# Attention followed by a feed-forward layer on one core: the attention output computed as token rows and transposed by TensorE, with a written-out program order

## The chip, the cores and the metric

The kernel runs on one core of one Trainium2 chip. The metric is device time in microseconds (us) of one execution. The kernel before takes 209.25 us, the median of three runs (209.20, 209.25 and 210.02 us).

## What is computed

The reference is a gated linear attention whose output goes through a feed-forward layer with a cosine gate. All arrays are float32: q, k, v and alpha have the shape (4, 8, 768, 48), that is 4 batches, 8 heads, 768 steps and 48 channels; w_in is 384 x 2048, w_out is 2048 x 384, and the result is 3072 x 384.

```python
for t in range(S):                                  # S = 768
    state = alpha[:, :, t, :, None] * state + einsum('bhd,bhe->bhde', k[:, :, t], v[:, :, t])
    y[:, :, t] = einsum('bhd,bhde->bhe', q[:, :, t], state)
x = y.transpose(0, 2, 1, 3).reshape(3072, 384)
h = x @ w_in
out = (h * cos(h)) @ w_out
```

## The kernel before

The 3072 tokens are cut into 24 chunks of 128; six chunks make one batch, and the attention state starts from nothing at chunks 0, 6, 12 and 18. Each chunk goes through the same small steps. The program has a one- or two-letter name for each step, and a string of such names with chunk numbers is the order in which the instructions of every engine are written. Each engine takes its own instructions strictly in that order, and waits where an operand or a buffer is not ready.

The steps of a chunk j are these. The names are used below.

- Loads on the SP queue: `a` (alpha), `k`, `q` and `v`, 192 KB each, in pieces of 192 bytes. Before, one step loads k and q together. `z` loads a part of w_in and `Z` a part of w_out.
- Decay: `l` (logarithm of alpha for two chunks, ACT), `C` (TensorE sums it along the chunk, L161 and L165), `E` (two exponentials, ACT, L179 and L181). `i`, `c` and `d` are the same for one chunk.
- Operands (GpSimd, shown as POOL): k times the inverse decay (L191, `khb`), q times the decay (L193, `qhb`), v cast to bfloat16 (L195, `vpb`), and a small decay mask (L197, `Em`). Before, one step `o` writes all four in this order.
- `T`: eight transposes of k and q on TensorE (L210); `t` copies them out of PSUM (DVE, L216).
- `A`: eight score matmuls, each on 48 rows of the array, alternately at row 0 and row 64 (L227); `m` masks them (DVE, L236).
- `S`: four matmuls for the chunk's contribution to the state (L249, 96 columns each); `u` adds the state before (DVE, L261) and multiplies by the decay (POOL, L263).
- `Y`: the attention output (L304). Before, the result is built transposed: v and the state are the weights, 64 columns of the array at a time, alternately in the left and the right half, and the scores or the transposed q stream through with 128 columns. That is 12 matmuls for the first chunk of a batch and 20 for the others. `y` copies the result out (DVE, L309) as `xT`, which the feed-forward layer reads.
- `F` and `G`: the two halves of x @ w_in, 24 matmuls each (L323); `f` and `g` the cosine on ACT (Sin of h + pi/2, L331); `p` and the gate of the second half multiply (DVE, L338).
- `V` and `W`: the two halves of the second matmul, 8 matmuls of 384 columns each (L347); `e` copies the result out (ACT, L363) and stores it.

PSUM has three pools. "big" has three buffers, of two banks each, for the sums of `C`, the scores and the halves `F` and `G`. "o" has one bank for the output of `V` and `W`. "g" has one single bank, which `T`, `S` and `Y` of every chunk use in turn, so that each of them waits until DVE has emptied the one before it:

```python
    def outputs(j):
        t = ps.tile([C, 512], FP, tag="g")
```

ACT holds either the table for logarithm and exponential or the one for Sin, and loads the other one when the order changes between them (L141 and L331).

The program has a written start (`START`, chunks 0 to 4) and then a loop with one fixed order per chunk. In the start, 63 matmuls on zeros (`warmup`, L370) fill waits of TensorE. w_in is loaded in two halves and w_out in two halves, and they are cast to bfloat16 by DVE (L121) and ACT (L119).

Of the kernel before, what the change touches and what calls it, by code (L numbers as in the profile page):

```python
# [9 lines left out]
FP = mybir.dt.float32  # L10
# [6 lines left out]
def kernel(  # L17
# [23 lines left out]
    VS = 112  # L41
# [4 lines left out]
    cpool = ctx.enter_context(tc.tile_pool(name="cpool", bufs=3))  # L46
# [55 lines left out]
    def load_qk(j):  # L102
        for nm, src, d in (("k_sb", k, k_t), ("q_sb", q, q_t)):
            t = inpool.tile([C, H, D], FP, tag=nm)
            nc.sync.dma_start(out=t, in_=rows(src, j))
            d[j] = t

    def load_v(j):
        t = inpool.tile([C, H, D], FP, tag="v_sb")
        nc.sync.dma_start(out=t, in_=rows(v, j))  # L110
        v_t[j] = t

    def load_w1(f0, f1):
        nc.sync.dma_start(out=w1f[:, :, f0:f1],
                          in_=moe_w_in[:, f0:f1].rearrange("(k p) f -> p k f", p=C))
# [7 lines left out]
    def cast_w1(half, eng, k0, k1):  # L123
        f = slice(half * (DF // 2), (half + 1) * (DF // 2))
        cast(eng, w1[:, k0:k1, f], w1f[:, k0:k1, f])

    def load_w2(f):
        nc.sync.dma_start(
            out=w2f[:, f : f + 8],
            in_=moe_w_out[f * C : (f + 8) * C, :].rearrange("(f p) n -> p f n", p=C),  # L130
        )

    def cast_w2(eng, f0, f1):
        cast(eng, w2[:, f0:f1], w2f[:, f0:f1])
# [52 lines left out]
    def operands(j, qeng):  # L187
        cp = cp_t[j // 2][:, j % 2]
        icp = icp_t[j // 2][:, j % 2]
        k_sb, q_sb, v_sb = k_t.pop(j), q_t.pop(j), v_t.pop(j)  # L190
        nc.gpsimd.tensor_tensor(out=khb[:, j % 3, :, 0:D], in0=k_sb,  # L191
                                in1=icp.rearrange("s (h d) -> s h d", h=H), op=ALU.mult)
        qeng.tensor_tensor(out=qhb[:, j % 3, :, 0:D], in0=q_sb,  # L193
                           in1=cp[:, 0:HD].rearrange("s (h d) -> s h d", h=H), op=ALU.mult)
        nc.gpsimd.tensor_copy(out=vpb[:, j % 3, :, 0:D], in_=v_sb)  # L195
# [75 lines left out]
    def outputs(j):  # L271
        t = ps.tile([C, 512], FP, tag="g")
        y_ps[j] = t
        first = j % NC == 0
        vs = vpb[:, j % 3].rearrange("s h e -> s (h e)")
        qT = qkT_t[j]

        U = ub[:, (j - 1) % 3].rearrange("r p e -> r (p e)")
        mms = []
        for T in range(2 * 3):  # L280
            g, tt = T // 3, T % 3
            a = []
            if not first:


                for p, c0 in (((0, 0),), ((0, 64), (1, 96)), ((1, 160),))[tt]:
                    c0 += 2 * C * g
                    a.append((U[:, c0 : c0 + 64],
                              qT[:, (NP + 2 * g + p) * C : (NP + 2 * g + p + 1) * C]))
            for r in range(2):  # L290
                h = 4 * g + (2 * tt + r + 1) // 2
                c0 = 4 * VS * g + 64 * (2 * tt + r)
                a.append((vs[:, c0 : c0 + 64], A_t[j][:, ACOL[h] * C : (ACOL[h] + 1) * C]))
            mms.append(a)
        for half in range(2):
            mms[half] = [
                (T // 2, i == 0, i == len(mms[T]) - 1) + m
                for T in range(half, 6, 2) for i, m in enumerate(mms[T])
            ]
        for i in range(max(len(mms[0]), len(mms[1]))):  # L300
            for half in range(2):
                if i < len(mms[half]):
                    kt, start, stop, lhsT, rhs = mms[half][i]
                    nc.tensor.matmul(t[64 * half : 64 * half + 64, kt * C : (kt + 1) * C],  # L304
                                     lhsT, rhs, start=start, stop=stop, skip_group_check=True)

    def ev_outputs(j):
        t = work.tile([C, 3, C], BF, tag="xT")
        nc.vector.tensor_copy(out=t.rearrange("r k t -> r (k t)"), in_=y_ps.pop(j)[:, 0 : 3 * C])  # L309
        x_t[j] = t  # L310
        qkT_t.pop(j)
        A_t.pop(j)

# [20 lines left out]
    def gate(j, half):  # L334
        if j not in g_t:
            g_new = moe.tile([C, NF, C], BF, tag="g_sb", bufs=4)
            g_t[j] = g_new
        nc.vector.tensor_tensor(out=g_t[j][:, half * HF : (half + 1) * HF],  # L338
                                in0=h_ps.pop((j, half)), in1=c_t.pop((j, half)), op=ALU.mult)

    def ff2(j, half, whole=True):
        if half == 0 or not whole:
            o_new = ps.tile([C, 512], FP, tag="g" if j == NCH - 1 else "o")
            o_ps[j] = o_new
        for f in range(HF):
            ft = half * HF + f
            nc.tensor.matmul(o_ps[j][:, 0:DM], g_t[j][:, ft], w2[:, ft],  # L347
                             start=(f == 0 and (half == 0 or not whole)),
                             stop=(f == HF - 1 and (half == 1 or not whole)))

    oh_t = {}

    def ev_first(j):
        oh = moe.tile([C, DM], FP, tag="oh", bufs=3)
        nc.scalar.activation(out=oh, in_=o_ps.pop(j)[:, 0:DM], func=AF.Copy)
        oh_t[j] = oh

    def ev_ff2(j):
        o_sb = moe.tile([C, DM], FP, tag="o_sb", bufs=3)
        if j in oh_t:  # L360
            nc.vector.tensor_tensor(out=o_sb, in0=o_ps.pop(j)[:, 0:DM], in1=oh_t.pop(j), op=ALU.add)
        else:
            nc.scalar.activation(out=o_sb, in_=o_ps.pop(j)[:, 0:DM], func=AF.Copy)  # L363
        g_t.pop(j)
        nc.sync.dma_start(out=out[j * C : (j + 1) * C, :], in_=o_sb)

    def warmup(n):
        w_ps = ps.tile([C, 512], FP, tag="o")
# [4 lines left out]
    dve, act_e, pool = nc.vector, nc.scalar, nc.gpsimd  # L373
    units = {

        "o": lambda j: operands(j, pool), "O": lambda j: operands(j, dve),
        "T": transposes, "t": ev_transposes, "S": state, "u": ev_state,
        "A": scores, "m": mask_scores, "Y": outputs, "y": ev_outputs,

        "F": lambda j: ff1(j, 0), "f": lambda j: act(j, 0), "p": lambda j: gate(j, 0),  # L380
        "G": lambda j: ff1(j, 1), "g": lambda j: act(j, 1), "q": lambda j: gate(j, 1),

        "V": lambda j: ff2(j, 0), "W": lambda j: ff2(j, 1, j not in oh_t), "e": ev_ff2,
        "X": lambda j: ff2(j, 0, False), "x": ev_first,

        "N": lambda g: lnset(), "l": lambda g: ln(2 * g, 2), "C": lambda g: cums(2 * g, 2),
        "E": lambda g: exps(2 * g, 2),
# [65 lines left out]
```

## Time and profile before

| | |
|---|---|
| median of three runs | 209.25 us |
| span of the profiled execution, first to last instruction | 208.2 us |
| time from the median that lies around the span | 1.05 us |
| instructions | 6187 |
| HBM read and written | 25.17 MB and 4.72 MB |
| TensorE matmuls at L323, L347, L304, L210, L227, L249 | 1152, 384, 448, 192, 192, 96 |

The profiled execution's own time is not listed beside its span, so the median of the runs stands for it. PE is TensorE's matmul side and PEld its weight loads, which overlap with matmuls. A busy time of PE counts matmuls that are in flight, so the distance between the starts of two neighbouring matmuls tells what one costs. In the profile most PSUM tiles are called "t".

### The profile page before, as it was taken

The numbers are of one execution on the slowest core, as the hardware profiler recorded it, in microseconds if no ns is written. First come the engines' busy times: TensorE is split into PE (matmuls) and PEld (weight loads), VectorE is DVE, ScalarE is ACT, GpSimd is POOL, SyncE is SP. The second block draws the span as 40 slices with busy tenths as digits, with TensorE's granted clock in tenths as the row PEclk, the third lists the DMA queues.
The fourth block names the chain that finished last, engine by engine and source line by source line (L and its number), as shares of the span: only waits on it lengthen the run. The fifth ranks groups of instructions, "written<-read, shape, count | busy, mean of one in ns | idle before, by whom it ended". The sixth has DMA issues, their size and how long they took to land.

```text
span 208.2 us, 6187 instructions
## 1 busy us (share of the span) xinstructions
PE 196.8 (95%) x2645; PEld 149.0 (72%) x2647; DVE 136.7 (66%) x163; ACT 130.4 (63%) x142; POOL 79.6 (38%) x124
## 2 busy tenths in 40 slices
PE   7996869899999999999999999999999999999982
PEld 2343558677787887877878787787878878787851
DVE  7106857799776668487686685766776776777320
ACT  2064594998964955955937839739659558434420
POOL 3005362485570371561730931912804617401000
PEclk9999997999999999999999999999999999999999
DMA  6999999999999377566765955874774461101112
GB/s 139 312 197 319 186 218 360 260 179 199 179 225 191 80 151 157 113 148 123 160 131 93 188 117 106 162 152 97 135 154 94 100 114 43 41 2 39 38 38 77
DMA packets 106204, 30.29 MB, mean 145 GB/s; under 512 B 100288, under 2 KB 105408, under 8 KB 106176
## 3 DMA queue, kind: packets, MB, share of 16 engines
q1 hardware_dynamic: 106176, 29.89, 66.6%
q8 instruction: 20, 0.33, 0.7%
q14 instruction: 8, 0.07, 0.1%
HBM read 25.17 MB, written 4.72 MB: 144 GB/s over the span
## 4 chain that ended last, share of the span: by engine, by line
PE 82%; DVE 6%; DMA 4%; issue 4%; POOL 1%; SPq 1%; ACT 0%; POOLq 0%; DVEq 0%; ACTq 0%
PE o_new L347 32%; PE t L323 29%; PE t L304 8%; PE t L210 5%; DMA t<-in_k_dram 4%; PE t L227 3%; PE t L249 2%; PE cum_new L161 1%; DVE w_114 L121 1%; DVE g_new L338 1%; DVE t L216 1%; DVE qhb L193 1%; PE cum_new L165 1%; DVE t L309 1%; DVE t L236 1%
## 5 line engine op out<-in xcount | busy, mean ns | idle before, releaser
L331 ACT ACTIVATE c_sb<-t,halfpi 128x1024 bf16<-128x1024 f32 x48 | 53.3, 1115 | 41.7 <-PE t L323 41.3
L323 PE MATMUL t<-t,w_114 128*128 128x128 bf16 x1152 | 72.6, 220 | 0.4 <-DVE g_new L338 0.4
L347 PE MATMUL o_new<-w_116,g_new 128*128 128x384 bf16 x384 | 70.2, 327 | 0.6 <-ACT o_sb L363 0.6
L323 PEld LDWEIGHTS <-w_114 128*128 128x128 bf16 x1152 | 67.9, 99 | 3.5 <-issue 0.5
L338 DVE TENSOR_TENSOR g_new<-t,c_sb 128x1024 bf16<-128x1024 f32 x48 | 58.4, 1219 | 15.2 <-ACT c_sb L331 14.7
L191 POOL TENSOR_TENSOR khb<-t,icp_new 128x384 bf16<-128x384 f32 x24 | 25.0, 1041 | 74.8 <-ACT icp_new L179 73.7
L347 PEld LDWEIGHTS <-g_new 128*128 128x128 bf16 x384 | 34.1, 98 | 24.2 <-issue 0.8
L263 POOL TENSOR_TENSOR ub<-sc,Em 128x384 bf16<-128x384 f32 x20 | 17.4, 870 | 33.1 <-DVE sc L261 33.1
L236 DVE TENSOR_TENSOR t<-t,mask_f 128x1024 bf16<-128x1024 f32 x24 | 29.2, 1215 | 0.0
L193 POOL TENSOR_TENSOR qhb<-t,cp_new 128x384 bf16<-128x384 f32 x22 | 22.0, 1000 | 0.0
L216 DVE COPY t<-t 128x1024 bf16<-128x1024 bf16 x24 | 16.5, 687 | 8.1 <-PE t L210 8.1
L309 DVE CAST t<-t 128x384 bf16<-128x384 f32 x24 | 13.3, 554 | 11.4 <-PE t L304 11.3
L363 ACT ACTIVATE o_sb<-o_new 128x384 f32<-128x384 f32 x22 | 10.7, 485 | 15.9 <-PE o_new L347 15.8
L261 DVE TENSOR_TENSOR sc<-t,ub 128x384 f32<-128x384 f32 x20 | 11.1, 557 | 13.8 <-PE t L249 13.8
L370 PE MATMUL w_ps<-warm 128*128 128x512 bf16 x61 | 17.3, 435 | 1.4 <-DVE warm L56 1.2
L331 ACT ACT_TABLE_LOAD x13 | 16.7, 1283 | 0.2
L141 ACT ACT_TABLE_LOAD x13 | 16.7, 1283 | 0.2
L304 PE MATMUL t<-t,vpb 128*64 128x128 bf16 x288 | 15.9, 222 | 0.2 <-DVE t L216 0.2
L179 ACT ACTIVATE icp_new<-cum_new 128x768 f32<-128x768 f32 (+1 forms) x13 | 9.8, 757 | 7.3 <-PE cum_new L165 7.3
L370 PEld LDWEIGHTS <-warm 128*128 128x128 bf16 x63 | 6.5, 109 | 10.4 <-issue 4.5
L304 PE MATMUL t<-t,ub 128*64 128x128 bf16 x160 | 13.0, 227 | 1.0 <-DVE t L216 0.8
L304 PEld LDWEIGHTS <-vpb 128*64 128x64 bf16 x288 | 13.1, 111 | 0.9 <-issue 0.4
(47 smaller groups left out, 152.9 us busy)
## 6 DMA issues: line engine op xcount, KB each, us to landing
a_new<-in_alpha_dram SPq DMA_DIRECT2D x24, 192.0 KB, 3.7
t<-in_v_dram SPq DMA_DIRECT2D x24, 192.0 KB, 4.3
t<-in_k_dram SPq DMA_DIRECT2D x24, 192.0 KB, 4.0
t<-in_q_dram SPq DMA_DIRECT2D x24, 192.0 KB, 4.3
out_dram<-o_sb SPq DMA_DIRECT2D x24, 192.0 KB, 2.0
w1f<-in_moe_w_in_dram SPq DMA_DIRECT2D x2, 1536.0 KB, 7.8
w2f<-in_moe_w_out_dram SPq DMA_DIRECT2D x2, 1536.0 KB, 10.3
```

The source lines that it names most:

```text
L141: nc.scalar.preload_act_table_set("natural_log_exp_and_others")
L191: nc.gpsimd.tensor_tensor(out=khb[:, j % 3, :, 0:D], in0=k_sb, in1=icp.rearrange("s (h d) -> s h d", h=H), op=ALU.mult)
L193: qeng.tensor_tensor(out=qhb[:, j % 3, :, 0:D], in0=q_sb, in1=cp[:, 0:HD].rearrange("s (h d) -> s h d", h=H), op=ALU.mult)
L216: nc.vector.tensor_copy(out=t, in_=qkT_ps.pop(j))
L236: nc.vector.tensor_tensor(out=t.rearrange("s (h t) -> s h t", h=H), in0=A_ps.pop(j).rearrange("s (h t) -> s h t", h=H), in1=mask_f.unsquee ...
L263: eng.tensor_tensor(out=ub[:, j % 3, :, 0:96].rearrange("r p (a e) -> r p a e", a=2), in0=sc.rearrange("r p (a e) -> r p a e", a=2), in1=E ...
L304: nc.tensor.matmul(t[64 * half : 64 * half + 64, kt * C : (kt + 1) * C], lhsT, rhs, start=start, stop=stop, skip_group_check=True)
L323: nc.tensor.matmul(t[:, f], w1[:, kk, ft * C : (ft + 1) * C], x_t[j][:, kk], start=(kk == 0), stop=(kk == 2))
L331: nc.scalar.activation(out=c_sb, in_=h_ps[j, half], func=AF.Sin, bias=halfpi, scale=1.0)
L338: nc.vector.tensor_tensor(out=g_t[j][:, half * HF : (half + 1) * HF], in0=h_ps.pop((j, half)), in1=c_t.pop((j, half)), op=ALU.mult)
L347: nc.tensor.matmul(o_ps[j][:, 0:DM], g_t[j][:, ft], w2[:, ft], start=(f == 0 and (half == 0 or not whole)), stop=(f == HF - 1 and (half == ...
L370: nc.tensor.matmul(w_ps, warm[:, 0:C], warm, start=True, stop=True)
```

## The change

**The attention output is built as token rows.** `Y` now has the scores (for the state part: the transposed q) as weights with all 128 columns of the array, and v or the state stream through: four matmuls of 96 columns for the state, which the first chunk of a batch leaves out, and eight of 48 columns for the heads. The result is a tile of 128 tokens by 384. `y` copies it out as bfloat16, a new step `D` transposes it in three pieces of 128 columns on TensorE into a further tile of the bank "g", and a new step `B` copies that out (DVE) as `xT`. v and the state keep no padding for 64-column slices, and the memset of `vpb` is gone.

**Loads and weights.** k, q, v and alpha are loaded by a step each. w_in and w_out come in four quarters each, with casts by quarter: w_in two thirds on DVE and one third on ACT, w_out's quarters alternately on DVE and ACT.

**Steps and order.** `operands` is split into four steps (`K`, `Q`, `b`, `E_`), `F`/`G` gates have a tile for each half, the special case that evacuated two half outputs apart is gone, the pool of the exponentials has four buffers in place of three, and the whole program is one string of 24 chunks of steps. The warm-up matmuls are 69, in one tile.

```diff
-    vpb = consts.tile([C, 3, H, VS], BF, tag="vpb")
-    nc.vector.memset(vpb, 0.0)
-    ub = consts.tile([C, 3, NP, C], BF, tag="ub")
+    vpb = consts.tile([C, 3, H, D], BF, tag="vpb")
+    ub = consts.tile([C, 3, NP, 96], BF, tag="ub")
...
-    cpool = ctx.enter_context(tc.tile_pool(name="cpool", bufs=3))
+    cpool = ctx.enter_context(tc.tile_pool(name="cpool", bufs=4))
...
+    def load(nm, src, d, j):
+        t = inpool.tile([C, H, D], FP, tag=nm)
+        nc.sync.dma_start(out=t, in_=rows(src, j))
+        d[j] = t
+    QF = DF // 4
+    def load_w1(h):
+        f = slice(h * QF, (h + 1) * QF)
+        nc.sync.dma_start(out=w1f[:, :, f], in_=moe_w_in[:, f].rearrange("(k p) f -> p k f", p=C))
...
+    def cast_w2(h):
+        cast((nc.vector, nc.scalar)[h % 2], w2[:, 4 * h : 4 * h + 4], w2f[:, 4 * h : 4 * h + 4])
...
+    def khat(j):
+        icp = icp_t[j // 2][:, j % 2]
+        nc.gpsimd.tensor_tensor(out=khb[:, j % 3, :, 0:D], in0=k_t.pop(j),
+                                in1=icp.rearrange("s (h d) -> s h d", h=H), op=ALU.mult)
+    def qhat(j):
...
+        eng = nc.vector if j < 2 else nc.gpsimd
...
+    def vcast(j):
+        nc.gpsimd.tensor_copy(out=vpb[:, j % 3, :, 0:D], in_=v_t.pop(j))
...
     def outputs(j):
         t = ps.tile([C, 512], FP, tag="g")
         y_ps[j] = t
         first = j % NC == 0
-        vs = vpb[:, j % 3].rearrange("s h e -> s (h e)")
         qT = qkT_t[j]
...
-                    nc.tensor.matmul(t[64 * half : 64 * half + 64, kt * C : (kt + 1) * C],
-                                     lhsT, rhs, start=start, stop=stop, skip_group_check=True)
+        for p in range(NP):
+            if not first:
+                nc.tensor.matmul(t[:, p * 96 : (p + 1) * 96], qT[:, (NP + p) * C : (NP + p + 1) * C],
+                                 ub[:, (j - 1) % 3, p], start=True, stop=False, skip_group_check=True)
+            for h in (2 * p, 2 * p + 1):
+                nc.tensor.matmul(t[:, h * D : (h + 1) * D], A_t[j][:, ACOL[h] * C : (ACOL[h] + 1) * C],
+                                 vpb[:, j % 3, h], start=first, stop=True, skip_group_check=True)
     def ev_outputs(j):
-        t = work.tile([C, 3, C], BF, tag="xT")
-        nc.vector.tensor_copy(out=t.rearrange("r k t -> r (k t)"), in_=y_ps.pop(j)[:, 0 : 3 * C])
-        x_t[j] = t
+        t = work.tile([C, HD], BF, tag="y_sb")
+        nc.vector.tensor_copy(out=t, in_=y_ps.pop(j)[:, 0:HD])
+        y_t[j] = t
...
+    def x_transposes(j):
+        t = ps.tile([C, 3, C], BF, tag="g")
+        y = y_t.pop(j)
+        for kt in range(3):
+            nc.tensor.transpose(t[:, kt], y[:, kt * C : (kt + 1) * C], ident_bf)
+        xT_ps[j] = t
+    def ev_x(j):
+        x = work.tile([C, 3, C], BF, tag="xT", bufs=3)
+        nc.vector.tensor_copy(out=x, in_=xT_ps.pop(j))
+        x_t[j] = x
...
+        g_new = moe.tile([C, HF, C], BF, tag="g%d_sb" % half, bufs=4)
...
-        "a0 v0 z0 k0 20 N0 i0 v1 a2 w20 w20 w6 c0 d0 O0 a1 a3 w9 S0 u0 T0 t0 i1 k1 z1 c1 10 d1 k2 "
...
+        "a0 i0 q0 q1 a1 c0 v0 d0 Q0 i1 w11 c1 d1 k0 k1 K0 w9 T0 t0 K1 a2 a3 w4 A0 v1 Q1 w1 T1 t1 b0 m0 w9 Y0 "
...
```

TensorE, the output step `Y` of a chunk that is not the first of its batch. Before, its first rows are weight loads and matmuls of the state (`ub`) and of v (`vpb`), 64 output partitions by 128 columns each:

```order
L304 LDWEIGHTS ub
L304 MATMUL t<-t,ub 64x128
L304 LDWEIGHTS ub
L304 MATMUL t<-t,ub 64x128
L304 LDWEIGHTS vpb
L304 MATMUL t<-t,vpb 64x128
```

Now the same place begins with the transposed q as weights ("t") and the state streaming, then the scores as weights (also "t") and v streaming:

```order
L279 LDWEIGHTS t
L279 MATMUL t<-ub,t 128x96
L282 LDWEIGHTS t
L282 MATMUL t<-vpb,t 128x48
L282 LDWEIGHTS t
L282 MATMUL t<-vpb,t 128x48
```

Three such pieces follow it, 12 matmuls in all in place of 20, and the three transposes of `D` come some steps later.

TensorE, the scores (`A`). Before, every chunk's scores stand alone: this is the end of one chunk's block, followed by a half of x @ w_in.

```order
L227 LDWEIGHTS t_778
L227 MATMUL t_787<-t_778 128x128
L323 LDWEIGHTS w1_114
L323 MATMUL t_802<-t_714,w1_114 128x128
```

Now the blocks of chunks 10 and 11 touch; the tile numbers change from the one to the other in the middle.

```order
L228 LDWEIGHTS t_1557
L228 MATMUL t_1608<-t_1557 128x128
L228 LDWEIGHTS t_1583
L228 MATMUL t_1618<-t_1583 128x128
```

Chunks 13 and 14, 18 to 20, and 22 and 23 touch in the same way; the others stand alone as before.

POOL, from the operands of chunk 1 on in the first microseconds. Before, each chunk's operands stand together, and the step `u` of a chunk (`ub`) comes between two of them:

```order
L191 TENSOR_TENSOR khb<-t,icp_new 128x8x48
L195 CAST vpb<-t 128x8x48
L197 TENSOR_TENSOR Em<-cp_new,m_109 128x8
L263 TENSOR_TENSOR ub<-sc,Em 128x4x96
L191 TENSOR_TENSOR khb<-t,icp_new 128x8x48
L193 TENSOR_TENSOR qhb<-t,cp_new 128x8x48
```

Now, from the first instruction that needs the exponentials of chunks 2 and 3 up to the one that lets chunk 4 be transposed, POOL has this row of work:

```order
L189 TENSOR_TENSOR qhb<-t,cp_new 128x8x48
L198 TENSOR_TENSOR Em<-cp_new,m_108 128x8 x2
L264 TENSOR_TENSOR ub<-sc,Em 128x384
L183 TENSOR_TENSOR khb<-t,icp_new 128x8x48
L193 CAST vpb<-t 128x384
L183 TENSOR_TENSOR khb<-t,icp_new 128x8x48
L264 TENSOR_TENSOR ub<-sc,Em 128x384
L189 TENSOR_TENSOR qhb<-t,cp_new 128x8x48 x2
L183 TENSOR_TENSOR khb<-t,icp_new 128x8x48
```

The first half of x @ w_in for chunk 0 stood behind the operands of chunk 1, and now stands behind those of chunk 4.

More of the change, by code (lines that the diff above doesn't have):

```diff
@@ L334, in gate @@
     def gate(j, half):
[L335 to L342, printed above, removed]
+        g_new = moe.tile([C, HF, C], BF, tag="g%d_sb" % half, bufs=4)
+        g_t[j, half] = g_new
+        nc.vector.tensor_tensor(out=g_new, in0=h_ps.pop((j, half)), in1=c_t.pop((j, half)), op=ALU.mult)
@@ L343, in ff2 @@
+    def ff2(j, half):
+        if half == 0:
             o_new = ps.tile([C, 512], FP, tag="g" if j == NCH - 1 else "o")
             o_ps[j] = o_new
+        g = g_t.pop((j, half))
         for f in range(HF):
[L346 to L356, printed above, removed]
+            nc.tensor.matmul(o_ps[j][:, 0:DM], g[:, f], w2[:, half * HF + f],
+                             start=(f == 0 and half == 0), stop=(f == HF - 1 and half == 1))
@@ L398, in run @@
[L398 to L404 removed]
[5 rows of a table removed]
[L410 to L424 removed]
+        "a": load_a, "k": lambda j: load("k_sb", k, k_t, j), "q": lambda j: load("q_sb", q, q_t, j),
```

122 lines of the change are left out of this document (30 added, 92 removed), and 30 rows, old and new, of tables (ORDER, START).

## The prediction

> **What bounds the kernel now.** The first view is the page: how busy the engines are, in 40 slices of 5.2 us, and which engines the chain of waits runs through.
>
> ```profile
> PE 196.8 (95%) x2645; PEld 149.0 (72%) x2647; DVE 136.7 (66%) x163; ACT 130.4 (63%) x142; POOL 79.6 (38%) x124
> PE   7996869899999999999999999999999999999982
> PEclk9999997999999999999999999999999999999999
> DMA  6999999999999377566765955874774461101112
> PE 82%; DVE 6%; DMA 4%; issue 4%; POOL 1%; SPq 1%; ACT 0%; POOLq 0%; DVEq 0%; ACTq 0%
> ```
>
> TensorE holds 82% of the chain, and its gaps lie in the first nine slices, where DMA is at its limit as well. The busy time by stretch, with the start and the end set apart:
>
> ```profile
> 0.00:25.00 25.00, 20.95 (x130) 9.58 (x132) 11.68 (x20) 9.01 (x13) 6.34 (x16) 1.00 1.02 236
> 25.00:47.00 22.00, 19.40 (x292) 16.08 (x293) 16.98 (x20) 18.76 (x19) 10.89 (x15) 0.92 0.98 248
> 47.00:193.00 146.00, 145.74 (x2134) 116.14 (x2132) 105.13 (x123) 98.44 (x106) 62.35 (x93) 1.00 0.62 124
> 193.00:208.20 15.20, 10.74 (x97) 7.21 (x95) 2.87 (x3) 4.19 (x6) 0.00 (x0) 1.00 0.14 52
> ```
>
> From 47 to 193 us TensorE never waits (145.74 of 146 us), and DVE, the next one, is at 72%. There, time falls only with TensorE's work. The chain in order of time gives that work: the sums for the decay come back every two chunks.
>
> ```profile
> 83.32 0.18 PE cum_new L161
> 98.08 0.18 PE cum_new L161
> ```
>
> Two chunks take 98.08 - 83.32 = 14.76 us, and 24 take 177.1. Four chunks have the shorter `Y` (0.22 us less, below), so all useful TensorE work is about 176.2 us. The other 208.2 - 176.2 = 32.0 us is start, waits and end.
>
> **The change, term 1: `Y` and `D`.** What a matmul costs is the distance between starts. Groups of equal matmuls give it: (time of the group - one's own duration) / (count - 1).
>
> ```profile
> 87.14 1.50 PE L323 MATMUL t<-t,w_114 128*128 128x128 bf16 x24
> 88.57 0.25 PE L304 MATMUL t<-t,ub 128*64 128x128 bf16 x2
> 89.25 1.48 PE L347 MATMUL o_new<-w_116,g_new 128*128 128x384 bf16 x8
> L323 PE MATMUL t<-t,w_114 128*128 128x128 bf16 x1152 | 72.6, 220 | 0.4 <-DVE g_new L338 0.4
> 73.88 0.68 PE t L304 x20
> 66.45 0.46 PE t L304 x12
> ```
>
> 128 columns cost (1.50 - 0.22) / 23 = 0.056 us. The 24 before `Y` thus end at 87.14 + 24 x 0.056 = 88.48; `V` starts at 89.25, so `Y` costs 0.77 us. Its 20 matmuls alone start within 0.58 us; about 0.1 us goes at the change into the half-width arrangement and 0.1 at the change back. The 12 of a first chunk cost 0.68 - 0.46 = 0.22 less: 0.55. For the new shapes there are neighbours:
>
> ```profile
> 98.11 0.24 PE L165 MATMUL cum_new<-ones_bf,lnab 128*128 128x1 bf16 x4
> L165 PE MATMUL cum_new<-ones_bf,lnab x96: 163/163/167, 14.6 to 171.6; 128*128 128x1 bf16 x96
> 85.23 0.33 PE L249 MATMUL t<-vpb,khb 128*128 128x96 bf16 x4
> L249 PE MATMUL t<-vpb,khb x96: 202/206/281, 17.2 to 187.7; 128*128 128x96 bf16 x96
> ```
>
> 96 columns cost (0.33 - 0.206) / 3 = 0.042 us, one column (0.24 - 0.163) / 3 = 0.025, both with a new full-width weight each time. 48 columns lie between; I take 0.025, since 96 columns at 0.42 ns each put 48 at 0.02, under that floor. The new `Y` is 4 x 0.042 + 8 x 0.025 = 0.37 us (0.50 at the upper end), 0.20 in a first chunk, and `D` is 3 x 0.056 = 0.17. Saved: 20 x (0.77 - 0.54) + 4 x (0.55 - 0.37) = **5.3 us**; with the upper end, 2.2.
>
> A rule speaks against this. The Trainium skill, "TensorE: Matmul & The Clock Gate", section "LDWEIGHTS (loading the stationary operand)", gives a weight load as its columns divided by 1.2, about 107 ns for 128. By it, an estimate, twelve loads would take 1.28 us and the change would lose some 16 us. The trace disagrees for short streams: full-width loads follow each other every 25 ns at L165.
>
> **Term 2: scores side by side.** `A` works on 48 rows at a time, and is an arrangement of its own.
>
> ```profile
> 85.50 0.40 PE L227 MATMUL t<-t 48*128 48x128 bf16 x8
> 85.83 1.47 PE L347 MATMUL o_new<-w_116,g_new 128*128 128x384 bf16 x8
> ```
>
> `S` should be over at 85.23 + 4 x 0.042 = 85.40, but `A` starts at 85.50. Its four pairs take 0.22, to 85.72, and `V` starts at 85.83. So a block pays 0.2 us for both changes. Five times two blocks touch now: **-1.0 us**. Useful work falls to 176.2 - 5.3 - 1.0 = 169.9 us.
>
> **Term 3: what DVE, ACT and POOL get.** `y` stays, `B` is new:
>
> ```profile
> L309 DVE CAST t<-t 128x384 bf16<-128x384 f32 x24 | 13.3, 554 | 11.4 <-PE t L304 11.3
> L216 DVE COPY t<-t 128x1024 bf16<-128x1024 bf16 x24 | 16.5, 687 | 8.1 <-PE t L210 8.1
> ```
>
> 1024 bfloat16 columns take 0.687 us; 384 take between 0.26 (in proportion) and 0.55 (as L309). I take 0.36: if bfloat16 streams at twice the rate of float32 and both have the same fixed part, the two rows give 0.155 us fixed and 0.00052 us a bfloat16 column. That puts DVE at 105.1 + 20 x 0.36, some 112 us in a stretch that shrinks to about 140: 80%. In the loop this lies beside TensorE's work, if each copy out of bank "g" comes in time. Between two users of "g" the new order has at least 1.3 us of other TensorE work in nearly every place (a half `F` or `V`), and a copy with its signals takes 0.2 + 0.69 + 0.06. From chunk 5 on I find only one place that is short: `m`, `u` and their signals, 2.0 us, against 1.5 us of `S`, `W` between the scores of chunk 5 and `T` of chunk 6. I allow 1.0 us in all. ACT's order has 16 table loads in place of 27, 14 us less, on an engine with 0% of the chain: nothing.
>
> **Term 4: the start.** Before, the first `F` starts at 25.18 us, after 3.7 us of useful work (4 sums of the decay at 0.26, 2 `T` at 0.45, 2 `A` at 0.42, 2 `S` at 0.17, one `Y`): 21.5 us lost. The end loses 208.2 - 204.3 = 3.9 after the last matmul, and 32.0 - 21.5 - 3.9 = 6.6 goes between.
>
> ```profile
> 25.18 2.84 PE L323 MATMUL t<-t,w_114 128*128 128x128 bf16 x48
> 198.95 5.36 PE L347 MATMUL o_new<-w_116,g_new 128*128 128x384 bf16 x32 [0.58 <-ACT o_sb L363]
> a_new<-in_alpha_dram SPq DMA_DIRECT2D x24, 192.0 KB, 3.7
> 1.19 13.38 PE L370 MATMUL w_ps<-warm 128*128 128x512 bf16 x46 [1.19 <-DVE warm L56]
> L236 DVE TENSOR_TENSOR t<-t,mask_f 128x1024 bf16<-128x1024 f32 x24 | 29.2, 1215 | 0.0
> L181 ACT ACTIVATE cp_new<-cum_new 128x776 f32<-128x776 f32 x11 | 9.0, 817 | 0.0
> L191 POOL TENSOR_TENSOR khb<-t,icp_new 128x384 bf16<-128x384 f32 x24 | 25.0, 1041 | 74.8 <-ACT icp_new L179 73.7
> L193 POOL TENSOR_TENSOR qhb<-t,cp_new 128x384 bf16<-128x384 f32 x22 | 22.0, 1000 | 0.0
> L263 POOL TENSOR_TENSOR ub<-sc,Em 128x384 bf16<-128x384 f32 x20 | 17.4, 870 | 33.1 <-DVE sc L261 33.1
> L195 POOL CAST vpb<-t 128x384 bf16<-128x384 f32 x24 | 12.8, 533 | 1.3 <-DMA t<-in_v_dram 1.3
> ```
>
> Afterwards alpha is no longer behind a weight cast on ACT. It lands at 0.7 + 3.7 = 4.4 us; logarithm 0.5, sum 0.5, 20 warm-ups at 13.38/46 = 0.29 and a second sum 0.3 bring `T` of chunk 0 to 11.5. Then one thing follows another: `T` and its copy 1.4, q of chunk 1 on DVE 1.2, `T` and copy 1.4, mask 1.2, `Y` and copy 1.0, `S` and the next sum 0.8, exponentials 0.2 + 1.6: 20.3 us. Now the POOL rows that are shown with the change: two masks `Em` at 0.2, three q at 1.0, two state products at 0.87, three k at 1.04 and a v at 0.53 make 0.4 + 3.0 + 1.74 + 3.12 + 0.53 = 8.8, to 29.1. One of its state products waits for `S` of chunk 2, which stands behind two `D` in bank "g": I add 1.0. Then `T` of chunk 4 0.5, its copy 0.9, 0.7 behind a mask on DVE, and two casts of 0.6 before the first `F`: **33.4 us**. By then 8.1 us of useful work is done (8 sums, 5 `T`, 5 `A`, 3 `S`, 3 `Y`, 2 `D`), so 25.3 us is lost.
>
> Next, DVE is the fuller queue. From the first `F` it has two masks, `y`, a cast, `B`, a gate, `u`, a cast and a gate, 7.6 us in order; `G` of chunk 1 needs that last gate's buffer, and TensorE has 6.1 us ahead of it (three `F`, a `G`, `D`, `S`, `Y`). That loses 1.5 us. Up to `F` of chunk 5 both queues hold 28.4 us, and I allow 2.8 in all (bounds 0 and the 6.6 of before). Lost: 25.3 + 2.8 + 1.0 + 3.9 = 33.0 us, about as much as before: the order earns nothing net.
>
> **The sum.** 169.9 + 33.0 = **202.9 us** of span, against 208.2. With the 1.05 us between the span and the runs' median: **203.9 us**.
>
> **The rivals.**
>
> *The start is shorter.* If POOL's row isn't the limit, DMA is: 21 tiles stand before the first two quarters of w_in. At some 190 GB/s, which slices 10 to 12 of the page show with small pieces, a tile takes 1.03 us, and the quarters at 350 GB/s 2.2 each: 2.5 + 21.6 + 4.4 = 28.5, with two casts 29.7, 3.7 us earlier. For it: the chain above counts every wait in full. It gives 200.2 us, and 197.4 if the 2.8 after it vanish too.
>
> ```profile
> GB/s 139 312 197 319 186 218 360 260 179 199 179 225 191 80 151 157 113 148 123 160 131 93 188 117 106 162 152 97 135 154 94 100 114 43 41 2 39 38 38 77
> 19.75 1.87 POOL L191 TENSOR_TENSOR khb<-t,icp_new 128x384 bf16<-128x384 f32 x1 [2.39 <-ACT icp_new L179]
> 32.71 3.60 PE L323 MATMUL t<-t,w_114 128*128 128x128 bf16 x48
> PE t L304 <- DVE t L216: 0.9, 2, 0.8
> ```
>
> *The start is longer.* POOL's first products can take 1.87 in place of 1.04 us while DVE casts; its eight products would take up to 6.6 us more. And TensorE's clock can drop: in slice 7 of before (0.7 granted), 48 matmuls took 3.60 us where 2.84 is usual. Three of the eight slowed and one such drop cost 2.5 + 0.8 us: 207.2 us.
>
> The Trainium skill, the same page, section "HAM oscillation — how this bites in real kernels", asks for no idle gap over about 3.4 us. The trace agrees only in part: the clock fell although TensorE's longest wait on another engine's work was 0.8 us, just ahead of that slice. By the rule the new start keeps its clock, since 49 warm-ups behind the first `T` fill its gaps.
>
> *Bank "g" decides, and it is slower than before.* Four steps a chunk go through one bank, and DVE at 80% has to empty it each time. If a copy stands behind a gate that isn't counted on, TensorE waits up to 1.2 us. The forecast gain is 209.25 - 203.9 = 5.35 us, 0.22 us a chunk: from that wait on it is gone, and at half a gate (0.6 us) a chunk it is 203.9 + 14.4 = 218 us. For it: `D` follows `y` and precedes `B`, two more trips through DVE. Against: the counted distances, and in the old loop three users of "g" cost nothing at 72%.
>
> *The change doesn't save what it says*: 48-column matmuls at 96 columns' price lose 24 x 8 x 0.017 = 3.3 us of the saving: 207.2 us.
>
> **How the numbers follow.** The forecast (201.5 to 206) has 0.50, a shorter start (under 201.5) 0.18, a longer start or dearer matmuls (206 to 208.2) 0.16, no change 0.06, bank "g" 0.10. A measurement of this kernel tells about 0.5%, 1.05 us, from no change. So faster 0.84, same 0.06, slower 0.10. The range from 198.5 to 208.5 leaves out some 5% below and 13% above.
>
> **What would show it.** Starts of the output matmuls 0.025 us apart, 0.37 us for `Y`, no gap of 0.1 us around it; 0.2 us between `A` blocks gone; the first `F` at 33 us; 99% TensorE from 65 us on. Wrong it would be if PE waits for DVE (L289, L303) appear in the middle, or if the first `F` comes after 36 us.

## The result, and the profile after

| | time, us | ratio to before |
|---|---|---|
| before | 209.26 median (209.2 to 210.02, 4 runs) | |
| changed | 201.33 median (200.76 to 201.9, 4 runs) | 0.9627, 95% interval 0.9582 to 0.9673 |
| changed, timed again later | 201.8 median (201.0 to 202.48, 6 runs) | 0.9657, 0.962 to 0.9694 |
| predicted | 203.9 (198.5 to 208.5) | |

The profiled execution of the changed kernel took 200.76 us, with a span of 198.7. Its page, in the lines that were shown of before:

```profile
PE 189.0 (95%) x2544; PEld 146.1 (74%) x2549; DVE 139.9 (70%) x186; ACT 117.5 (59%) x133; POOL 78.5 (39%) x124
PE   1999998999999999999999999999999999999993
PEclk9999999999999999999999999999999999999999
DMA  6999999999988999999969945930915431111012
PE 66%; DMA 13%; SPq 11%; DVE 4%; POOL 3%; issue 2%; POOLq 0%; ACT 0%; DVEq 0%
```

The gaps of TensorE are gone from the second slice on, but a row of nines says less here than it seems: the 69 matmuls on zeros (64 of them have a record) count as busy. DMA and its queue (SPq) now hold 24% of the chain, nearly all of it before 62 us. The windows part the span at the first `F` (31.98), at the `F` of chunk 5 (62.46) and near the end; their columns are the length, the busy time of PE, PEld, DVE, ACT and POOL, the granted clock, the DMA share and GB/s.

```profile
0.00:31.98 31.98, 25.95 (x233) 13.59 (x238) 15.89 (x30) 12.90 (x19) 13.99 (x30) 1.00 1.13 211
31.98:62.46 30.48, 29.95 (x429) 24.46 (x431) 24.77 (x32) 22.16 (x25) 10.41 (x14) 1.00 0.97 243
62.46:195.00 132.54, 132.46 (x1880) 107.81 (x1878) 98.69 (x124) 81.90 (x90) 53.24 (x80) 1.00 0.60 120
195.00:198.70 3.70, 0.68 (x7) 0.28 (x4) 0.56 (x1) 0.49 (x1) 0.83 (x1) 1.00 0.15 53
```

From 62.46 to 195 us TensorE works 132.46 of 132.54 us. DVE stands at 98.69 / 132.54 = 74%. TensorE waits for nothing there, so bank "g" costs nothing either. What the new `Y` and `D` cost is read from TensorE's timeline (start, duration, instructions):

```profile
41.83 0.21 PE L279 MATMUL t<-ub,t 128*128 128x96 bf16 x1
41.87 0.21 PE L282 MATMUL t<-vpb,t 128*128 128x48 bf16 x2
41.93 0.20 PE L279 MATMUL t<-ub,t 128*128 128x96 bf16 x1
...
42.16 0.21 PE L282 MATMUL t<-vpb,t 128*128 128x48 bf16 x2
42.21 1.50 PE L315 MATMUL t<-x,w 128*128 128x128 bf16 x24
43.74 0.34 PE L298 MATMUL t<-ident_bf,t 128*128 128x128 bf16 x3
43.92 1.50 PE L315 MATMUL t<-x,w 128*128 128x128 bf16 x24
```

`Y` runs from 41.83 to 42.21, 0.38 us, with no gap of 0.1 us ahead of it or behind it. With 0.042 us for each of the four with 96 columns, one of 48 columns costs (0.38 - 0.17) / 8 = 0.026. `D` takes 0.18. A first chunk's `Y` is eight matmuls of 48 columns alone, and gives the distance directly, from its group (mean 183 ns) and its block on the timeline:

```profile
L282 PE MATMUL t<-vpb,t 128*128 128x48 bf16 x192 | 11.3, 183 | 0.0
```

```profile
106.73 0.36 PE L282 MATMUL t<-vpb,t 128*128 128x48 bf16 x8
107.03 0.62 PE L228 MATMUL t<-t 48*128 48x128 bf16 x16
107.58 1.51 PE L315 MATMUL t<-x,w 128*128 128x128 bf16 x24
```

(0.36 - 0.183) / 7 = 0.025 us. The Trainium skill, "TensorE: Matmul & The Clock Gate", section "Wait — 56ns, not 53.3ns?", says that starts never come closer than about 25 ns however few columns stream; the trace agrees, with a new full-width weight each time.

### The profile page after: what moved, and what is told of

Same layout as the page of the kernel before. It is cut to its first block, busy times and chain, and to the rows that moved or that the text cites. A ratio compares the mean times of both kernels' runs of the same rounds, so it can differ in the third digit from the quotient of the medians.

```text
span 198.7 us, 5949 instructions
## 1 busy us (share of the span) xinstructions
PE 189.0 (95%) x2544; PEld 146.1 (74%) x2549; DVE 139.9 (70%) x186; ACT 117.5 (59%) x133; POOL 78.5 (39%) x124
## 4 chain that ended last, share of the span: by engine, by line
PE 66%; DMA 13%; SPq 11%; DVE 4%; POOL 3%; issue 2%; POOLq 0%; ACT 0%; DVEq 0%
PE o_new L337 26%; PE t L315 25%; DMA t<-in_k_dram 7%; SPq L102 7%; PE t L211 4%; DMA w1f<-in_moe_w_in_dram 4%; SPq L98 4%; PE t L228 2%; PE t L250 2%; PE t L282 2%; DMA t<-in_q_dram 2%; PE t L298 2%; DVE g_new L329 1%; PE t L279 1%; POOL khb L183 1%
## 5 line engine op out<-in xcount | busy, mean ns | idle before, releaser
L315 PE MATMUL t<-x,w 128*128 128x128 bf16 x1152 | 71.2, 219 | 0.9 <-DVE w L115 0.9
L337 PE MATMUL o_new<-w,g_new 128*128 128x384 bf16 x384 | 69.4, 326 | 0.1
L315 PEld LDWEIGHTS <-w 128*128 128x128 bf16 x1152 | 65.5, 98 | 1.6 <-DVE w L115 1.2
L337 PEld LDWEIGHTS <-g_new 128*128 128x128 bf16 x384 | 35.3, 98 | 20.0 <-issue 0.5
L183 POOL TENSOR_TENSOR khb<-t,icp_new 128x384 bf16<-128x384 f32 x24 | 23.9, 1000 | 25.1 <-DMA t<-in_k_dram 24.5
L353 PE MATMUL w_new<-warm 128*128 128x512 bf16 x64 | 18.6, 422 | 0.3 <-issue 0.2
L193 POOL CAST vpb<-t 128x384 bf16<-128x384 f32 x24 | 12.5, 522 | 6.2 <-DMA t<-in_v_dram 6.1
L142 ACT ACTIVATE lnab<-a_new 128x768 bf16<-128x768 f32 (+1 forms) x13 | 10.1, 792 | 4.9 <-DMA a_new<-in_alpha_dram 4.9
L303 DVE COPY x<-t 128x384 bf16<-128x384 bf16 x24 | 8.4, 351 | 6.5 <-PE t L298 6.5
L155 PE MATMUL cum_new<-lnab,triu_bf 128*128 128x384 bf16 x24 | 7.3, 334 | 4.3 <-ACT lnab L142 4.3
L282 PE MATMUL t<-vpb,t 128*128 128x48 bf16 x192 | 11.3, 183 | 0.0
```

Of the source, the lines that this page charges most:

```text
L183: nc.gpsimd.tensor_tensor(out=khb[:, j % 3, :, 0:D], in0=k_t.pop(j), in1=icp.rearrange("s (h d) -> s h d", h=H), op=ALU.mult)
L282: nc.tensor.matmul(t[:, h * D : (h + 1) * D], A_t[j][:, ACOL[h] * C : (ACOL[h] + 1) * C], vpb[:, j % 3, h], start=first, stop=True, skip_g ...
L315: nc.tensor.matmul(t[:, f], w1[:, kk, ft * C : (ft + 1) * C], x_t[j][:, kk], start=(kk == 0), stop=(kk == 2))
L337: nc.tensor.matmul(o_ps[j][:, 0:DM], g[:, f], w2[:, half * HF + f], start=(f == 0 and half == 0), stop=(f == HF - 1 and half == 1))
L353: nc.tensor.matmul(w_ps, warm[:, 0:C], warm, start=True, stop=True)
```

## The experiments

Chip times are set against the kernel before on the same chip, whose median lay between 208.74 and 209.11 us. Names of steps are those used above. The first four part the change into its two halves, the form of `Y` with `D`, and the order.

### The old form in the new order

The changed kernel with the functions of before for `Y` and `y` (and the padded tiles that they need); `D` and `B` do nothing.

```diff
-        "D": x_transposes, "B": ev_x,
+        "D": lambda j: None, "B": lambda j: None,
```

> The new order with the old form of the output: Y again with 64-column slices (12 or 20 matmuls), D and B left out, everything else as in the changed kernel. Theory 'form' (a full-width Y with its transposes saves 0.23 us a chunk, 5.3 us in all, and nothing waits for D and B): 201.3 + 5.3 = 206.6 us, between 205.5 and 208. Rival 'order' (the written-out order earns the gain, the form little or nothing): under 203 us.

Measured: 205.94 us (205.19 to 207.41), ratio 0.9833 (0.9793 to 0.9873). So the new form is worth 205.94 - 201.33 = 4.6 us in the new order (4.1 against the later timing), and the order, with all the rest of the change (weights in quarters, split operands, buffers), some 3 us. The middle gives the form's part without the start's scatter. By the starts of the halves of x @ w_in, counted after the first one, the ninth and the last stand at

```
                      half 9    half 47   between
changed kernel         60.68     188.65    127.97
old form, new order    63.48     195.15    131.67
```

and 17 `Y` lie between, two of them of first chunks: 15 x 0.23 + 2 x 0.18 = 3.81 by the prediction's prices, 3.70 measured.

### The new form in the old order

The kernel before with the new functions. `D` and `B` are put behind each `y`, with one half of a matmul or the scores between. In the loop `Y` moves ahead of `V`, so that `V` stands between `Y` and `D`:

```diff
-        run(f"V{V} G{s} g{s} p{s} Y{s + 1} y{s + 1} q{s}")
+        run(f"G{s} g{s} p{s} Y{s + 1} y{s + 1} V{V} D{s + 1} q{s} B{s + 1}")
```

> The old order with the new form of the output, D and B placed with matmuls of other steps between Y, D and the next T (in the loop Y goes ahead of V, D stands between V and W; in the start one step lies between). Theory 'form': 209.3 - 5.3 = 204.0 us, between 203 and 205. Rival 'order': over 207 us. Rival 'bank g' (four users of the one bank make TensorE wait for DVE): 209 us or more, with PE waiting for the copies of y and B in the middle of the trace.

Measured: 217.26 us (217.19 to 217.43), ratio 1.0388 (1.036 to 1.0416). The expectation from the form alone fell, by 13 us. The time is what the rival of bank "g" expected, but the wait that the trace shows is only in part the one it named: the same arithmetic that earns 4.6 us in one order loses 8 in the other. Two lines of the waits (total, times, longest):

```profile
PEld L295 <- DVE t L286: 8.7, 22, 0.9
PEld L279 <- DVE t L234: 3.2, 16, 0.2
```

And one chunk of the loop on the timeline, DVE first and then `V` and `D` on PE:

```profile
92.66 1.23 DVE L327 TENSOR_TENSOR g_new<-t,c_sb 128x1024 bf16<-128x1024 f32 x1 [0.30 <-ACT c_sb L320]
93.80 0.55 DVE L286 CAST t<-t 128x384 bf16<-128x384 f32 x1
...
92.76 1.46 PE L336 MATMUL o_new<-w,g_new 128*128 128x384 bf16 x8
94.40 0.34 PE L295 MATMUL t<-ident_bf,t 128*128 128x128 bf16 x3 [0.19 <-DVE t L286]
```

`Y` was over at 92.76, when `V` began, but its copy (L286) stands behind a gate of 1.23 us on DVE and starts at 93.80; `D` (L295) waits for it, though a whole `V` of 1.3 us lies between. The weight loads of 22 of the 24 `D` wait, 0.40 us each on average. `D` reads what this copy writes, so it would wait for it with a bank of its own too: the wait shows the price of one more trip through DVE, not that of the shared bank.

### The same with everything side by side

`Y y D B` in one piece, everywhere, with the loop's order otherwise as before.

```diff
-        run(f"V{V} G{s} g{s} p{s} Y{s + 1} y{s + 1} q{s}")
+        run(f"V{V} G{s} g{s} p{s} Y{s + 1} y{s + 1} D{s + 1} B{s + 1} q{s}")
```

> As the run before, but D stands directly behind Y on TensorE and B directly behind y on DVE, in the loop as in the start. Theory 'bank g decides by distance': D waits for the signal, the copy of y and the signal back, 0.2 + 0.55 + 0.06 = 0.8 us where DVE is free and up to 2.0 us where a gate stands ahead, so 24 x 0.8 to 2.0 = 19 to 48 us more than with distance: 223 to 250 us. If the bank costs nothing however close its users stand: 204 us.

Measured: 226.21 us (226.03 to 226.35), ratio 1.0814 (1.0784 to 1.0843), inside the range expected.

```profile
PEld L295 <- DVE t L286: 18.0, 22, 1.2
PE t L295 <- DVE t L286: 15.7, 22, 1.1
```

The wait per chunk is 18.0 / 22 = 0.82 us, twice the 0.40 with a `V` between, and TensorE stands idle for it. The Trainium skill, "Perfetto Trace Analysis", section "Matmuls" under "Optimizing Tensor Performance", wants independent groups of matmuls to rotate through PSUM banks, so that the copy of one lies beside the next. No run here shows that: `Y` and `D` of one chunk are not independent, since the copy between them makes what `D` reads, and a second bank for `D` wasn't tried.

### A control: the old form with that move of `Y`

```diff
-        run(f"V{V} G{s} g{s} p{s} Y{s + 1} y{s + 1} q{s}")
+        run(f"G{s} g{s} p{s} Y{s + 1} y{s + 1} V{V} q{s}")
```

> The kernel before with one thing moved: in the loop Y stands ahead of V, as in the run with the new form. A control for that move. Theory: TensorE has the same work and waits for nothing new, 209.3 us within 1 us. If the move itself earns or costs something: outside 208.3 to 210.3.

Measured: 210.32 us (209.1 to 211.83, 10 runs), ratio 1.0061 (1.0024 to 1.0098). The move itself costs some 0.6%, so against the same order the new form loses 217.26 - 210.32 = 6.9 us, where term 1 of the prediction had it gain 5.3. Most of it lies in the written start: the eighth half of x @ w_in after the first begins at 58.78 us with the new form and at 52.34 with the old one. Not all of these 6.4 us is the form's. The first `F` already stands 1.7 us later (25.67 against 23.96), and between the new form in the old order and the copies-first kernel below (24.61), which have the same start, it moves by 1.1 us by itself. From there to the eighth half TensorE is idle for 6.3 us against 3.5, and its granted clock is 0.95 over 33.1 us against 1.00, by estimate 1.7 us.

### The copies ahead of the gates

The new form in the old order again, TensorE's order untouched. In the loop, DVE makes the copy `y` ahead of the gate `p`, and `B` ahead of the second gate:

```diff
-        run(f"G{s} g{s} p{s} Y{s + 1} y{s + 1} V{V} D{s + 1} q{s} B{s + 1}")
+        run(f"G{s} g{s} Y{s + 1} y{s + 1} p{s} V{V} D{s + 1} B{s + 1} q{s}")
```

> The second experiment's kernel (new form, old order) with two things moved on DVE alone, in the loop: the copy y stands ahead of the first gate p, and the copy B ahead of the gate q. TensorE's order is the same. Theory 'a copy of bank g that stands behind a gate makes TensorE wait': the waits of D for y (0.16 to 0.6 us a chunk there) go, 0.3 to 0.5 us a chunk over 18 chunks of the loop, 5 to 9 us less than 217.3: 208 to 212 us; what is left over 204 is lost in the start. Rival (the place of the copies among the gates doesn't matter, the fourth step in the bank does): 217.3 us within 1.5, or more where the gates come late.

Measured: 213.3 us (212.56 to 213.84), ratio 1.0235 (1.0162 to 1.0309), 4.0 us less than with the gates first. That is 1.3 us above the range expected, but the mechanism shows in its waits and its timeline:

```profile
PEld L295 <- DVE t L286: 1.6, 3, 0.9
```

```profile
91.06 0.56 DVE L286 CAST t<-t 128x384 bf16<-128x384 f32 x1 [0.59 <-PE t L279]
91.53 1.22 DVE L327 TENSOR_TENSOR g_new<-t,c_sb 128x1024 bf16<-128x1024 f32 x1
...
92.16 0.33 PE L295 MATMUL t<-ident_bf,t 128*128 128x128 bf16 x3
```

The copy now comes at 91.06 and the gate behind it, and `D` follows `V` without a wait; three of 24 still wait, in the start. Twelve chunks of the loop take 87.7 us in place of 90.2. From the eighth half, where the loop begins, to the end it is 210.8 - 57.40 = 153.4 us in place of 215.5 - 58.78 = 156.7, so 3.3 us come from the two moves; the rest of the 4.0 lies in the start, which they leave as it was. With the gates first and the old form (the control above) that stretch took 207.5 - 52.34 = 155.2, so in the loop the new form with its copies first wins 1.8 us. So the order of two instructions on DVE decides the loop's part. The rest of the loss is the written start (the eighth half at 57.40 us, 54.59 in before), which wasn't rearranged, and a wait of 0.2 us for the mask inside each `Y` (the L234 line above).

### The scores pulled apart

In the new order, the five places where two `A` touch get another step between them, like this one:

```diff
-        "... W9 Y12 E8 A13 k17 E_14 k18 k19 e9 A14 ..."
+        "... W9 E8 A13 Y12 k17 E_14 k18 k19 e9 A14 ..."
```

> The changed kernel with the score blocks of chunks 10/11, 13/14, 18/19/20 and 22/23 pulled apart by one other TensorE step each (a state, an output, a transpose or a half of the second matmul), so that all 24 stand alone. Theory: each of the five touches saves 0.2 us of arrangement changes, so 201.3 + 1.0 = 202.3 us, within 0.5. Rival (the changes of arrangement overlap with something): 201.3 us within 0.5.

Measured: 202.4 us (202.09 to 202.78), ratio 0.9677 (0.965 to 0.9704): 1.07 above the changed kernel, 1.0 expected (0.6 above its later timing). A pair (`L228`, 16 matmuls) stands in the last timeline of the changed kernel above. A single block looks like this; it is that of chunk 9, which stands alone in both kernels, from the timeline of the one pulled apart:

```profile
81.33 0.33 PE L298 MATMUL t<-ident_bf,t 128*128 128x128 bf16 x3
81.59 0.40 PE L228 MATMUL t<-t 48*128 48x128 bf16 x8
81.92 0.34 PE L155 MATMUL cum_new<-lnab,triu_bf 128*128 128x384 bf16 x1
```

From the end of what stands ahead (106.73 + 8 x 0.025 = 106.93, and 81.33 + 3 x 0.056 = 81.50) to the next start a pair takes 0.65 us and a single block 0.42: 0.19 saved a pair. Chunks 13 and 14, pulled apart, take 0.42 and 0.44 in the same way. Half 9 to half 47 takes 129.21 us in place of 127.97, 1.24 more for five.

### The weights two tiles later

Two loads, v of chunk 3 and q of chunk 5, go ahead of the first quarters of w_in on the SP queue.

```diff
-        "... t4 z0 s0 A3 w2 A4 z1 r1 v3 Y2 ... s3 q5 u3 ..."
+        "... t4 v3 q5 z0 s0 A3 w2 A4 z1 r1 Y2 ... s3 u3 ..."
```

> The changed kernel with two input tiles (v of chunk 3, q of chunk 5) loaded ahead of the first two quarters of w_in, not behind them. Theory 'DMA sets the first F' (DVE's cast waited 0.7 us for the second quarter): the first F comes 2 x 1.0 = 2.1 us later, at 34 us, and the time is 202.3 to 203.4 us. Rival 'POOL's row sets it' (as predicted): the first F within 0.7 us of 32.0, and the time within 0.7 us of 201.3.

Measured: 204.46 us (203.8 to 204.89), ratio 0.9772 (0.9742 to 0.9802). The first row is the cast of w_in's first quarters on DVE's timeline in the changed kernel, the second the same cast here, and the third the window from the first `F` on here (its last columns: granted clock, DMA share, GB/s):

```profile
30.63 1.29 DVE L115 CAST w<-w1f 128x1024 bf16<-128x1024 f32 x2 [0.73 <-DMA w1f<-in_moe_w_in_dram]
```

```profile
33.05 1.30 DVE L115 CAST w<-w1f 128x1024 bf16<-128x1024 f32 x2 [3.77 <-DMA w1f<-in_moe_w_in_dram]
```

```profile
34.41:46.59 12.18, 12.16 (x181) 11.59 (x182) 10.15 (x14) 7.35 (x9) 3.51 (x4) 0.82 0.91 277
```

The cast moves by 2.42 us and the first `F` by 34.41 - 31.98 = 2.43, so the transfer sets the start. That explains 2.4 of the 3.1 us. The rest, which takes the time beyond the expected 203.4 us, wasn't foreseen: the granted clock is 0.82 for 12 us, after TensorE had waited 4.0 us for that cast.

### No warm-ups behind the first `T`

All 49 `w` behind the first `T` are left out.

```diff
-        "... T0 t0 K1 a2 a3 w4 A0 v1 Q1 w1 T1 t1 b0 m0 w9 Y0 ..."
+        "... T0 t0 K1 a2 a3 A0 v1 Q1 T1 t1 b0 m0 Y0 ..."
```

> The changed kernel without the 49 warm-up matmuls behind the first T. Theory 'they hold the clock': TensorE's granted clock falls in the first slices, the matmuls of the first F run at up to twice the distance for some 3 us, and the time is 202.5 to 204.5 us. Rival 'they only fill, or are in the way': 201.3 us or up to 0.7 us less.

Measured: 202.73 us (202.25 to 203.37), ratio 0.9702 (0.9671 to 0.9733): 1.4 us lost.

From the page, the windows and the waits of this kernel:

```profile
PEclk9995555999999999999999999999999999999999
```

```profile
12.00:32.94 20.94, 12.91 (x153) 9.48 (x153) 11.89 (x19) 8.24 (x12) 9.67 (x17) 0.58 1.14 247
```

```profile
PE cum_new L155 <- ACT lnab L142: 1.9, 1, 1.9
```

The clock falls to half for four slices, with TensorE busy for 12.91 of 20.94 us and no wait longer than 1.9 us. The first `F` comes at 32.94 us, only 0.96 later: the cast ahead of it now starts at 31.59 and waits for no transfer, so the slowed TensorE has become what is last, after it had used up the 0.7 us for which the cast had waited for the transfer.

### The last states left out, and the changed kernel again

`S`, `u` and `E_` of chunks 5, 11, 17 and 23 compute a state that no later chunk reads. This kernel leaves them out. Two more, timed side by side with the changed kernel as it is, leave out those of 11, 17 and 23, and again all four.

```diff
-        "... V2 m6 S5 K7 u5 W2 ..."
+        "... V2 m6 K7 W2 ..."
```

> The changed kernel without the state steps (S, u and the decay mask) of chunks 5, 11, 17 and 23, whose results no later chunk reads. A try for a better version. Theory 'TensorE's work is the time': 4 x 0.17 = 0.7 us less, 200.6 us. If the bank g or DVE also limits: up to 2 us less.

Measured: 200.9 us (200.53 to 201.24), ratio 0.9604 (0.9576 to 0.9631). The interval overlaps with the changed kernel's, so three kernels were timed side by side, six times each:

> The changed kernel as it is, timed again beside the two others of this job, so that differences of half a per cent can be told. Every theory expects 201.3 us (200.8 to 201.9).

> The changed kernel without the state steps S, u and E_ of chunks 11, 17 and 23, whose results nobody reads; those of chunk 5 are kept. Theory 'saved work counts in the full middle': two S of 0.17 us ahead of the last half, and one after it that ends the program after the last result, so 0.3 us of PE and the tail: 200.7 us, and the stretch up to 62 us stays as it is. Rival 'the order is tuned as a whole': the stretch between chunks 5 and 6 stays, but another wait takes the gain: 201.3 or more.

> The same without all four state steps (5, 11, 17 and 23), timed again beside the other two. Theory 'saved work counts': 0.1 to 0.2 us below the one that keeps chunk 5's, 200.6 us. Rival: the wait of 1.3 us for q of a later chunk, seen between 47 and 61 us when chunk 5's steps went, comes back every time and eats what is saved, so this one is no faster than the one that keeps them: 200.9 us or more.

Measured: 201.8 us (201.0 to 202.48) as it is, 200.66 (200.0 to 201.52) with chunk 5's kept, 200.66 (200.16 to 201.88) without all four; ratios to before 0.9657, 0.9608 and 0.9611. Between the means of the first two lies 1.0 us, with a 95% interval of 0.2 to 1.8 from the scatter of the six runs each. So leaving them out beats the changed kernel, by a little. Half 9 to half 47 takes 127.81, 127.47 and 127.48 us, which shows 0.3 us of it; the rest of the 1.0 may be scatter of the start. Whether chunk 5's are kept made no difference. The wait of 1.3 us for q between 47 and 61 us in the first run without all four was 0.2 in the next profile of the same kernel, so the rival built on it, that it comes back every time, fell.

The same cast as above explains the scatter of the start. First the changed kernel again, then the one that keeps chunk 5's, then the first one without all four:

```profile
31.15 1.29 DVE L115 CAST w<-w1f 128x1024 bf16<-128x1024 f32 x2 [1.86 <-DMA w1f<-in_moe_w_in_dram]
```

```profile
30.43 1.30 DVE L115 CAST w<-w1f 128x1024 bf16<-128x1024 f32 x2 [0.44 <-DMA w1f<-in_moe_w_in_dram]
```

```profile
29.91 1.30 DVE L115 CAST w<-w1f 128x1024 bf16<-128x1024 f32 x2
```

The first `F` starts at 32.50, 31.78 and 31.27 us, 1.35 or 1.36 behind the cast each time, as with 30.63 and 33.05 above. In the last one the transfer was early and the cast waited for nothing but its own queue: the other limit lies only 0.7 us below.

## Why the prediction was right, and where not

The direction was right, so were the mechanisms of terms 1 and 2, and the time lies in the range, 2.6 us below the forecast. By the prediction's own parts it is a case of the shorter start (under 201.5, chance 0.18), the later timing of 201.8 just one of the forecast (0.50). The span came out 4.2 us shorter (198.7 against 202.9); the time around the span was 2.06 us in place of 1.05; and the profiled execution of the changed kernel was 0.57 below the median. -4.2 + 1.0 + 0.57 = -2.6. It is luck that the last two took back part of the first. Of the span's 4.2 us, 3.6 are lost time, worked out below under term 4, and the rest lies in the useful work.

**Term 1, `Y` and `D`: right.** 0.38 us for `Y` (0.37 predicted), 0.18 for `D` (0.17), 3.70 us for 17 chunks (3.81); in whole runs 4.6 of 5.3. The rival "the change doesn't save what it says" is out, and so is the estimate that weight loads would make the change lose 16 us.

**Term 2, the scores: right.** 1.07 us by the runs and 1.24 by the traces, 1.0 predicted.

**Term 3: the copies right, the waits not.** `B` has its own row in the groups of the changed kernel (busy, mean ns, idle before):

```profile
L303 DVE COPY x<-t 128x384 bf16<-128x384 bf16 x24 | 8.4, 351 | 6.5 <-PE t L298 6.5
```

0.351 us against 0.36, and DVE at 74% where I had 80%. I allowed 1.0 us for waits on bank "g" from chunk 5 on, and there were none.

**Term 4, the start: mis-sized, and this is the step that failed.** It ended in "the order earns nothing net". Lost time (all that isn't useful work on TensorE):

| us | before | predicted | measured |
|---|---|---|---|
| up to the first `F`, less 8.1 of work | 21.5 | 25.3 | 31.98 - 8.1 = 23.9 |
| from there to `F` of chunk 5, less 28.4 of work | 6.6 (to the end of the middle) | 2.8 | 30.48 - 28.4 = 2.1 |
| middle | | 1.0 | 0 |
| end, after the last matmul of an output | 3.9 | 3.9 | 198.70 - 195.35 = 3.35 |
| sum | 32.0 | 33.0 | 29.4 |

The order thus wins 2.6 us of lost time, besides the 1.0 of the scores, and the old form in the new order, 3.0 us faster than before, shows about the same: some 0.8 of the 2.6 only says that the profiled execution of before, with its span of 208.2 us, was a longer one. About 1 us of what whole runs gain goes with the clock, which the prediction left unnamed in the 6.6 us of before. Of the 37 executions of before that were timed beside the experiments, the 6 with a granted clock of 0.999 or 1.000 took 207.50 to 207.77 us and the 31 with 0.991 or 0.992 took 208.49 to 210.08, while every execution of the changed kernel had at least 0.998. I had worked out the start as a row on POOL that ends at 29.1, with 1.0 for a wait and 3.3 behind it. The measured row (start and duration on POOL) ends earlier:

```profile
27.49 1.01 POOL L183 TENSOR_TENSOR khb<-t,icp_new 128x384 bf16<-128x384 f32 x1
```

28.5 in place of 30.1 us, one product after another at 1.0 as priced, but started by exponentials at 19.6 and with shorter waits. Then not POOL but the second quarter of w_in was last, which landed at 23.11 + 7.49 = 30.6, by the chain in order of time:

```profile
23.11 7.49 DMA w1f<-in_moe_w_in_dram
```

So the rival "the start is shorter", in which DMA sets it, held, at 31.98 in place of its 29.7, and the two limits lie 0.7 us apart. That rival was right about the place; its two transfers, priced at 4.4 us, ended 7.5 us after the issue at 23.11. (Its 190 GB/s for the small tiles is a misreading: slices 10 to 12 show 199, 179 and 225, which would put it another 1.1 us earlier. The 21 tiles were issued by 22.3 us, about 1.0 us each; whether the queue or the transfers set that pace isn't shown.)

**The time around the span** was taken as 209.25 - 208.2 = 1.05. A later run of before with a span of 207.2 took 208.96, so 1.8; the profiled execution had simply been slower than the median. A span and a median of different executions shouldn't have been subtracted.

**The rivals.** "The start is longer" did not come about: POOL's products took 1.0 us, and the clock stayed at 1.00 in the profiled execution. "Bank g decides, slower than before" did not come about in this kernel, but it was no idle rival: in the old order the times were 217 and 226 us. Its point of decision, a copy behind a gate that wasn't counted on, was right, and moving the copies ahead of the gates alone won 4.0 us, 3.3 of them in the loop. That the bank is the reason is not shown: `D` waits for the copy whose result it reads. What kept the changed kernel clear of it is its order; the form put into the old order was a loss of 8 us, the clock's part in it included.

## What to carry to other kernels

A new arrangement of matmuls that needs one more trip through PSUM is to be priced together with the order of the engine that makes the copy: here the same form earned 4.6 us or lost 8, and moving two copies ahead of two gates on DVE was worth 3.3 us in the loop. Where the start is a race of several queues, write down each one's end, not the likeliest alone: POOL and DMA were 0.7 us apart, and only the later one counts. Take span and total from the same execution.

## What the runs showed that I had not expected

**The clock after a wait.** The granted clock fell in whole slices after waits that were short: 0.58 over 21 us with no wait over 1.9 us (no warm-ups), and 0.82 over 12 us after one of 4.0 us. In the changed kernel again and in the second profile without all four states TensorE waited 2.0 us each time at the first `F`; the first kept its clock there, and the second lost it in one slice:

```profile
PEclk9999997999999999999999999999999999999999
```

The Trainium skill, "TensorE: Matmul & The Clock Gate", section "HAM oscillation — how this bites in real kernels", puts the limit at an idle gap of about 3.4 us. The runs don't agree with it as a limit for one gap: several gaps of 0.5 to 1.9 us did the same.

Which waits cost the clock can be read off the 14 traces. In each of them the granted clock is 1.00 or 0.50 and changes only at whole multiples of 3.41 us, counted from its first rise. Cut into pieces of that length, each of the 17 pieces at full clock in which PE was busy for at most 1.887 us was followed by half the clock, and none of the 772 others (1.892 us and more) was. The two profiles with a wait of 2.0 us differ in where it fell: in the one that lost its clock the piece from 28.69 to 32.11 us has 1.88 us of busy time, in the other the wait is split between two pieces, with 2.09 and 2.69 us. So short waits add up within a piece. This was read from the traces afterwards, with PE's modelled ends; no experiment was made to test it.

**A quarter of a per cent from a transfer.** The same kernel's first `F` stood at 31.98 and at 32.50 us in its two profiles, by the landing of one weight quarter. That is 0.52 of the 1.2 us between the two executions (200.76 and 201.96); all its runs lie between 200.76 and 202.48.
